# The loads of a fused attention and GELU kernel as steps of their own, and a new order for every block

## The chip, the cores and the metric

The kernel runs on one NeuronCore of a Trainium2 chip. A core has five engines, each with an instruction queue of its own that runs in order: TensorE (PE in the profile; its weight loads are a row of their own, PEld), VectorE (DVE), ScalarE (ACT), GpSimd (POOL) and SyncE (SP). [...]Transfers between HBM and the on-chip memory SBUF run on 16 DMA engines. SP, ACT and POOL issue them: here SP the stores and the transposing loads, POOL the loads that change the type from float32 to bfloat16. The metric is the device time of one execution in microseconds (us), lower is better.

## The reference

Cross-covariance attention over channels, followed by a feed-forward layer with a tanh GELU. There are 4 batches of 6080 tokens with 256 channels; the hidden width is 2048.

```python
qn = q / (np.linalg.norm(q, axis=1, keepdims=True) + 1e-06)      # per channel, over all tokens
kn = k / (np.linalg.norm(k, axis=1, keepdims=True) + 1e-06)
s = kn.transpose(0, 2, 1) @ qn / tau                              # 256 x 256 for each batch
a = softmax(s)                                                    # over the last axis
x = (v @ a).reshape(B * S, D)
h = x @ w_in
g = 0.5 * h * (1.0 + np.tanh(c * (h + 0.044715 * h * h * h)))
out = g @ w_out
```

All the tokens of a batch must have passed through q and k before the first output of that batch can be made.

## The kernel before

The 256 x 256 matrix a is first multiplied into w_in, so each batch has one 256 x 2048 weight AW = a @ w_in (`aw_part`, lines 428 to 436, and `aw_copy`, 438 to 447; steps `aw0` to `aw7` and `ac0` to `ac7`). Then every batch has 12 blocks of 512 tokens (the last has 448), 48 blocks in all. A block n does this:

- v reaches the core in two transfers: `cast_v` (line 133) has POOL copy the float32 rows to a bfloat16 scratch tile `vb` in HBM, and `load_vt` (143) has SP load that transposed into `vT`, one of three buffers.
- h = AW.T @ vT, in pairs of 128-channel slices. Two to eight of the eight pairs are made directly (`mm1`, 484, step `g0` to `g7`: four matmuls of 512 columns into a pair of PSUM banks) and turned into GELU values by ACT (`gelu`, 502, `G0` to `G7`). The other pairs are made two at a time in sets `w0`, `w1`, `w2` by seven half-size products in place of eight (a Strassen scheme; `small`, 542, `w0m1` to `w0m7`), with sums of v made by DVE (`sums_v`, 526, `vs`) and sums of AW (`sums_w`, 513, `SW0` to `SW2`), and copies and additions around them (`set_step`, 580). Blocks 0 and 1 use no set, block 2 one, blocks 3 to 35 two, blocks 36 to 47 three.
- out = g @ w_out, by the same scheme: seven products, each in two halves (`product`, 682, `M1A` to `M7B`), sums of the GELU values by DVE (`sums_1`, 658, `T1a`; `sums_2`, 664, `T2a` to `T4b`), sums of w_out made once at the start (`prep_wout`, 630, `pA11` to `pNA`), additions (`cq`, `y5`, `ap`, `ax`, `c11a`), four turns from columns to rows (`c11`, `c12`, `c21`, `c22`, 719). With the fourth turn of a block SP is given its store, four transfers (782). The last block is stored in halves, `sA` and `sB` (771), from SP and ACT.

While batch b runs its blocks, q and k of batch b + 1 are brought in and reduced, in 8 chunks: `load_one` (95) loads one chunk of q or of k by POOL into one of five buffers; `qsq` and `ksq` (`square`, 167) square it on ACT; `f1` (`fold`, 198) halves the squares on DVE, and `fd` (`fold_dma`, 206) has POOL add them into an accumulator by DMA; `row0` to `row5` (`gram_row`, 217) are the matmuls of k against q. Late in the batch the norms, the softmax and the new AW follow as steps (`fl1`, `gc`, `ss`, `sv`, `pow`, `kf`, `kr`, `krp`, `S0`, `th0`, `dn`, `rc0`, `eT`, `rsum`, `rs`). The first batch's q and k are worked through ahead of the blocks, in the order of lines 794 to 854.

Nothing is scheduled by the framework. Lines 929 to 932 walk through `ORDER[WINDOW[n]]` for each block n, and issue each step as it stands in the text; `-1` and `+1` behind a step name the neighbouring block that it belongs to. This text fixes the order in every engine's queue. `WINDOW` has 48 entries and `ORDER` 31 texts: blocks 8 to 19 and 20 to 33 share texts, as do four blocks near the end.

The transfers hang on three markers in each text, `e0`, `e2` and `e5`, which call `loads` (911): `e0` issues the transpose of block n + 2 and the cast of block n + 3, `e2` the chunk of q with the block's own number in the batch, `e5` the same chunk of k. A gate (`GATE`, 500; `after`, 89) makes each of POOL's loads wait for the last `mm1` or `small` matmul issued ahead of it. Chunk c is so loaded in block c of a batch, and its first `row` or square stands in the next block, for a few chunks in the one after.

Of the kernel before, what the change touches and what calls it, by code (L numbers as in the profile page):

```python
# [18 lines left out]
def kernel(  # L19
# [26 lines left out]
    PE_BLOCKS = 2  # L46
# [611 lines left out]
    def sums_1(n):  # L658
        hc = cols_of(n) // 2
        t1 = t1p.tile([128, 8, BLK // 2], BF16, tag="t1", name=f"t1_{n}")  # L660
        nc.vector.tensor_sub(t1[:, :, :hc], quarter(n, 0, 1), quarter(n, 0, 0))
        TS[n] = {1: t1}

    def sums_2(n, i, half):
        hc = cols_of(n) // 2
        ts = TS[n]
# [127 lines left out]
    with tc.manual_schedule():  # L794
# [78 lines left out]
        def step(what, n):  # L873
# [30 lines left out]
            elif what[0] == "p":  # L904
                prep_wout(what)
            elif what[0] == "e":
                loads(n, int(what[1]))
            else:
                mm2_step(n, what)

        def loads(n, p):
            b, blk = divmod(n, NB)
            gate = GATE[0]
            if p == 0 and PE_BLOCKS <= n + 2 < NN:
                load_vt(n + 2)
            if p == 0 and n + 3 < NN:
                cast_v(n + 3, gate)
            if p in (2, 5) and b + 1 < B and blk < len(chunks_of(b + 1)):
                load_one(b + 1, blk, p // 5, gate)
# [16 lines left out]
    0, 1, 2, 3, 4, 5, 6, 7, 8, 9, 10, 11, 12, 13, 14, 15, 16, 17, 18, 19, 8, 9, 10, 11,  # L936
    12, 13, 14, 15, 16, 17, 18, 19, 8, 9, 20, 21, 22, 23, 24, 25, 26, 27, 27, 27, 27, 28,
    29, 30,
]
ORDER = [  # L940
    """aw4 aw5 aw3 g1 ac3 ac5 aw2 G1 g0 ac2 e0 aw7 G0 g3 ac7 ac4 g2 G3 SW0 e2 aw6 G2 g5 ac6 g4
    T1a G5 vtp G4 g7 vtc1 vtc0 e5 w0m1+2 pA11 G7 g6 pF0 M1A G6 M1B pS1 g1+1 pA12 pF1""",
    """g0 G1 e0 M5B-1 T2a-1 G0 M5A-1 T2b-1 g3 e2 pS2-1 cq-1 g2 T4b-1 G3 T3a-1 M6B-1 G2 M6A-1
    pS3-1 g5 e5 y5-1 ap-1 g4 G5 T3b-1 M7A-1 G4 vs+1 row4 g7 pS4-1 g6 G7 T4a-1 M7B-1 G6 M3A-1
    T1a w0m5+1 row0 w0cq+1 M3B-1""",
    """g0 w0y5 c12-2 ax-2 pNA-2 e0 w0m6 row5-1 w0ap row2-1 M2A-2 qsq M2B-2 w0m2 e2 c11a-2 w0m7
    w0m3 T2b-1 M4B-2 w0Gq M4A-2 w0ax M5A-1 T3a-1 G0 row3-1 M5B-1 T4b-1 w0m4 w0Gx g4 c21-2 w0Gr
    SW1-2 e5 g3 G4 T2a-1 w0m1+1 M1A-1 c22-2 G3 T3b-1 M1B-1 g6 cq-1 y5-1 ksq-1 M6A-1 M6B-1 g5
    ap-1 G6 T1a M3A-1 M7B-1 G5 T4a-1 M7A-1 M3B-1 ksq row1-1 c12-1 g7 ax-1 vs+1 M2A-1 G7 M2B-1
    c11-2 w0m5+1 T2a row2 w0cq+1 M4A-1 T3a M4B-1 w0y5+1 c11a-1 w0m6+1 qsq-1""",  # L950
    """g0 w0ap e0 c21-2 row1-1 w0m7 G0 w0m3 w0ax M1B-1 M1A-1 T2b-1 w0Gx e2 w0m4 row0-1 w0Gr g3
    T4b-1 cq-1 c22-2 w0m2 f1-2 G3 M5A-1 M6A-1 c11-2 M5B-1 fd-2 w0Gq vs+1 w1m1 w1m5 e5 M6B-1
    y5-1 w1cq g4 ap-1 w1y5 T3b-1 w1m6 G4 M3B-1 w1ap M7B-1 row5-1 ksq w1m7 g7 w1ax T1a w1m2 G7
    M3A-1 row4-1 w1m4 w1m3 c12-1 w1Gr M7A-1 w0m5+1 w1Gq ax-1 M2B-1 f1-1 row3-1 w0m1+1 w1Gx
    M2A-1 T4a-1 w0cq+1""",
    """g0 fd-2 T2b-1 w0y5 e0 w0m6 G0 M4A-2 w0ap M4B-2 row3 qsq-1 c21-2 w0m7 g3 e2 w0ax T2a-1 w0m3
    G3 M1B-1 c11a-2 row5 w0m2 T4a-1 row0-1 qsq row4-1 w0m4 T3b-1 M1A-1 vs+1 M5B-1 w0Gr row4 e5
    w1m5 T4b-1 w0Gq row0 row2-1 w1m1 M5A-1 cq-1 row5-1 w1cq g4 w1y5 w1m6 w0Gx M6A-1 w1ap G4
    M6B-1 c22-2 row3-1 w1m7 T3a-1 w1m2 y5-1 w1m3 g7 ap-1 w1Gq w1ax M7A-1 T1a G7 M3B-1 w1m4
    row1-1 w1Gx M7B-1 w1Gr M3A-1 w0m5+1 ksq c12-1""",  # L960
    """g0 T2a-1 e0 w0m1 ax-2 row4 w0cq M2B-2 f1-2 M2A-2 w0y5 row2-1 c11-3 fd-2 G0 w0m6 e2 row2
# [168 lines left out]
```

## Time and profile before

| | |
|---|---|
| median of 13 runs | 716.08 us (710.86 to 721.09) |
| the profiled execution | 721.09 us, the slowest of the 13 |
| its span, first to last instruction | 719.3 us |
| mean granted TensorE clock | 0.989 |
| TensorE busy | 94% of the span |
| ACT, DVE busy | 86%, 85% |
| POOL busy | 13% |
| DMA engines, mean rate | 137 GB/s |

The page of a profile lists the busy time of each engine, the costliest groups of instructions (line, engine, operation, output tile <- input tiles, shape, count, busy time and mean duration in ns), the idle time ahead of a group and what ended it, and the chain of work that ended last, followed back from the last instruction. A timeline gives the instructions of one engine in order: start, length, instruction, and in brackets the idle time before it with its releaser. A matmul on two tiles reads `out<-moving,weights`. `G`, `r`, `p`, `h`, `rb`, `qp` are PSUM tiles: `G` the matrix of k against q, `h` a direct pair, `rb` and `qp` the products of a set, `r` and `p` those of the second layer. `t` is a chunk of q or k, `acc` the accumulator of squares, `ot` a block's output.

The 40 slices of the span show where TensorE is not full:

```profile
PE   3868989998999999999999999999999999999995
DVE  4574867986999878888999878897899999999996
ACT  5356979997888999999888999999888999999993
PEclk9998999999999999999999999999999999999999
DMA  9995697998647899999627797999734736463414
```

Each digit stands for some 18 us, in tenths. The orders begin in the third slice, at about 39 us; the first two are the first batch's q and k. The blocks of batches 0 to 2, up to about 515 us, carry the loads of the next batch in their first eight blocks, and there DMA is high.

### The profile page before, as it was taken

What the parts mean: (1) busy time and instruction counts of PE and PEld (TensorE: products, weight loads), DVE (VectorE), ACT (ScalarE), POOL (GpSimd) and SP (SyncE); (2) the same over time, 40 slices, a digit from 0 to 9 for tenths busy, and PEclk for the clock granted to TensorE, in tenths of its full rate; (3) what the DMA queues carried; (4) which work ended last, traced back from release to release, by engine and by line L of the source; (5) the groups of instructions that cost most, each with busy time, mean ns of one, the idle gap of its engine ahead of it and who ended that gap; (6) DMA issues with size and microseconds to landing.
All of it is one profiled execution on the core that took longest, in us unless ns stands there. A gap on an engine that the chain in (4) does not pass through costs nothing.

```text
span 719.3 us, 14365 instructions
## 1 busy us (share of the span) xinstructions
PE 679.5 (94%) x5479; PEld 531.5 (74%) x5479; DVE 609.0 (85%) x1180; ACT 619.0 (86%) x894; POOL 92.0 (13%) x155
## 2 busy tenths in 40 slices
PE   3868989998999999999999999999999999999995
PEld 2635757785777877777777778777777888888884
DVE  4574867986999878888999878897899999999996
ACT  5356979997888999999888999999888999999993
POOL 4310111121100111121100011112010000000000
PEclk9998999999999999999999999999999999999999
DMA  9995697998647899999627797999734736463414
GB/s 242 208 241 84 99 178 153 204 174 169 116 69 107 148 176 162 223 176 200 124 50 109 136 201 142 188 201 194 150 60 67 109 58 97 80 117 59 73 31 86
DMA packets 165734, 98.21 MB, mean 137 GB/s; under 512 B 150848, under 2 KB 153664, under 8 KB 164672
## 3 DMA queue, kind: packets, MB, share of 16 engines
q0 software_dynamic: 16896, 58.34, 43.2%
q1 hardware_dynamic: 147664, 37.67, 31.3%
q10 hardware_dynamic: 1104, 1.28, 0.5%
q8 instruction: 43, 0.70, 0.4%
q14 instruction: 27, 0.22, 0.1%
HBM read 78.91 MB, written 36.83 MB: 161 GB/s over the span
## 4 chain that ended last, share of the span: by engine, by line
PE 81%; DMA 9%; issue 7%; POOL 1%; DVE 1%; ACT 0%; POOLq 0%; DVEq 0%
PE r L700 21%; PE h L494 17%; PE p L700 16%; PE rb L570 12%; PE qp L570 9%; DMA t<-in_k_dram 7%; PE G L225 4%; PE awp L434 1%; DMA t<-in_q_dram 1%; POOL t L99 1%; POOL vb L138 0%; PE ss L257 0%; POOL wst L622 0%; PE rk L379 0%; DVE a L191 0%
## 5 line engine op out<-in xcount | busy, mean ns | idle before, releaser
L700 PEld LDWEIGHTS <-wcomb 128*128 128x128 bf16 x2688 | 263.3, 98 | 44.8 <-issue 1.7
L504 ACT ACTIVATE g<-h 128x1024 bf16<-128x1024 f32 (+1 forms) x178 | 179.3, 1014 | 34.6 <-PE h L494 32.3
L494 PE MATMUL h<-vT,aw 128*128 128x512 bf16 (+1 forms) x648 | 165.0, 378 | 0.0
L700 PE MATMUL r<-t,wcomb 128*128 128x256 bf16 (+1 forms) x1152 | 164.7, 271 | 0.3 <-DVE c L716 0.2
L596 ACT ACTIVATE g<-qp 128x1024 bf16<-128x1024 f32 (+1 forms) x103 | 104.5, 1016 | 6.1 <-PE qp L570 4.7
L494 PEld LDWEIGHTS <-aw 128*128 128x128 bf16 x712 | 70.2, 99 | 50.3 <-issue 1.9
L700 PE MATMUL p<-g,wcomb 128*128 128x256 bf16 (+1 forms) x760 | 104.6, 272 | 0.0
L570 PEld LDWEIGHTS <-sw 128*128 128x128 bf16 x824 | 80.7, 98 | 21.2 <-issue 0.6
L178 ACT ACTIVATE sq<-t 128x1536 bf16<-128x1536 bf16 (+4 forms) x60 | 80.8, 1358 | 13.0 <-DMA t<-in_q_dram 9.8
L591 DVE TENSOR_TENSOR qp<-rb,yw 128x512 f32<-128x512 f32 (+1 forms) x103 | 71.1, 690 | 20.8 <-PE rb L570 10.4
L594 DVE TENSOR_TENSOR xw<-rb,yw 128x512 f32<-128x512 f32 (+1 forms) x103 | 69.7, 677 | 20.5 <-PE rb L570 18.6
L570 PE MATMUL rb<-tv,sw 128*128 128x256 bf16 (+1 forms) x412 | 78.5, 273 | 0.0
L570 PEld LDWEIGHTS <-aw 128*128 128x128 bf16 x618 | 60.1, 98 | 23.2 <-issue 8.5
L225 PE MATMUL G<-t 128*128 128x256 bf16 (+1 forms) x368 | 62.2, 276 | 10.5 <-DMA t<-in_k_dram 10.5
L673 DVE TENSOR_TENSOR t<-g,t 128x1024 bf16<-128x1024 bf16 (+1 forms) x96 | 63.5, 672 | 7.6 <-ACT g L504 6.4
L586 ACT ACTIVATE qp<-rb 128x512 f32<-128x512 f32 (+1 forms) x103 | 60.3, 585 | 10.5 <-PE rb L570 5.3
L138 POOL DMA_DIRECT2D vb<-in_v_dram x46 | 25.0, 544 | 330.4 <-PE h L494 280.4
L589 ACT ACTIVATE yw<-qp 128x512 f32<-128x512 f32 (+1 forms) x103 | 61.1, 593 | 4.6 <-PE qp L570 2.1
L675 DVE TENSOR_TENSOR t<-g 128x1024 bf16<-128x1024 bf16 (+1 forms) x96 | 64.2, 671 | 0.2
L677 DVE TENSOR_TENSOR t<-t,g 128x1024 bf16<-128x1024 bf16 (+1 forms) x96 | 64.0, 670 | 0.0
L604 ACT ACTIVATE g<-xw 128x512 bf16<-128x512 f32 (+1 forms) x103 | 63.1, 624 | 0.2 <-DVE xw L594 0.2
L601 ACT ACTIVATE g<-rb 128x512 bf16<-128x512 f32 (+1 forms) x103 | 61.3, 596 | 1.8 <-PE rb L570 0.9
(122 smaller groups left out, 901.5 us busy)
## 6 DMA issues: line engine op xcount, KB each, us to landing
out_dram<-ot SPq DMA_DIRECT2D x176, 128.0 KB, 3.1
acc<-a POOLq DMA_DIRECT2D x24, 768.0 KB, 7.0
vb<-in_v_dram POOLq DMA_DIRECT2D x42, 256.0 KB, 4.7
t<-in_q_dram POOLq DMA_DIRECT2D x22, 384.0 KB, 6.5
t<-in_k_dram POOLq DMA_DIRECT2D x22, 384.0 KB, 6.5
wst<-in_moe_w_out_dram POOLq DMA_DIRECT2D x2, 1024.0 KB, 11.4
t<-in_q_dram POOLq DMA_DIRECT2D x3, 512.0 KB, 15.1
t<-in_k_dram POOLq DMA_DIRECT2D x3, 512.0 KB, 17.0
```

The source lines that it names most:

```text
L178: nc.scalar.activation(o, t[:np_, r, :], AF.Square)
L225: nc.tensor.matmul(G[b][:, jc, :], lhsT=qt[:np_, r, jc * 128 : jc * 128 + 128], rhs=kt[:np_, r, :], start=first and jc == 0, stop=jc == 1, ...
L494: mm = nc.tensor.matmul(hp[:, u, :cols], lhsT=AW[b][:, cc, fc * 128 : fc * 128 + 128], rhs=vt_tiles[n][:, cc, :cols], start=cc == 0, stop= ...
L504: nc.scalar.activation(gs(n)[:, 2 * p : 2 * p + 2, :cols], HP.pop((n, p))[:, :, :cols], AF.Gelu_apprx_tanh)
L570: GATE[0] = nc.tensor.matmul(acc[:, u * hc : u * hc + hc], lhsT=lhs[:, u * 128 : u * 128 + 128], rhs=rhs, start=m in (1, 5) and u == 0, st ...
L591: nc.vector.tensor_add(qp(n, i)[:, 1, :c], RB[n, i][:, :c], YW[n, i][:, :c])
L594: nc.vector.tensor_add(XW[n, i][:, :c], RB[n, i][:, :c], YW.pop((n, i))[:, :c])
L596: nc.scalar.activation(gs(n)[:, 2 * pa : 2 * pa + 2, :c].rearrange("p u (t x) -> p t u x", t=2), QP.pop((n, i))[:, :, :c].rearrange("p t ( ...
L673: nc.vector.tensor_sub(o, quarter(n, 1, 1, f0, f1), ts[1][:, f0:f1, :hc])
L675: nc.vector.tensor_sub(o, quarter(n, 1, 1, f0, f1), quarter(n, 0, 1, f0, f1))
L677: nc.vector.tensor_sub(o, ts[2][:, f0:f1, :hc], quarter(n, 1, 0, f0, f1))
L700: nc.tensor.matmul(ACCS[n, acc][:, :hc], lhsT=wcomb[:, w, fc, :], rhs=x, start=first and k == 0, stop=k == 3, skip_group_check=True)
```

## The change

The markers and `loads` go. In their place are four steps with a block number like any other: `lt` (transpose of v), `lv` (cast of v), `lq` and `lk` (a chunk of q, of k). With a block number m of the batch, `lq` and `lk` load chunk m - 1 of the next batch; `lq+2` in block n is so chunk n + 1, where before it was chunk n. Batch 1's chunks 0 to 3 are loaded in the same blocks as before (written `+1`), the `lq` of chunk 4 follows in block 3, its `lk` and chunk 5 in block 4, chunk 6 in block 5, chunk 7 in block 6. For batches 2 and 3, chunk 0 is loaded in the block ahead of the ones that carried the loads before (blocks 11 and 23), chunk 7 in blocks 18 and 30. `lq` stands about a third, `lk` about two thirds into a block; `lt+2` and `lv+3` stay near its start. The gates stay.

All other steps are the same, one by one, but every block has a text of its own now, and so another order. Block 0 begins with `aw2 aw3 g0` in place of `aw4 aw5 aw3 g1` and no longer reads block 2's `vT`; the sums of w_out begin at its end. The end of block 47 is another. Two lines allow `T3a` ahead of `T1a` of its block.

```diff
     def sums_1(n):
...
-        TS[n] = {1: t1}
+        TS.setdefault(n, {})[1] = t1
     def sums_2(n, i, half):
...
-        ts = TS[n]
+        ts = TS.setdefault(n, {})
...
-            elif what[0] == "e":
-                loads(n, int(what[1]))
+            elif what == "lt":
+                load_vt(n)
+            elif what == "lv":
+                cast_v(n, GATE[0])
+            elif what in ("lq", "lk"):
+                load_one(b, c, "qk".index(what[1]), GATE[0])
...
-        def loads(n, p):
-            b, blk = divmod(n, NB)
-            gate = GATE[0]
-            if p == 0 and PE_BLOCKS <= n + 2 < NN:
-                load_vt(n + 2)
-            if p == 0 and n + 3 < NN:
-                cast_v(n + 3, gate)
-            if p in (2, 5) and b + 1 < B and blk < len(chunks_of(b + 1)):
-                load_one(b + 1, blk, p // 5, gate)
...
 WINDOW = [
-    0, 1, 2, 3, 4, 5, 6, 7, 8, 9, 10, 11, 12, 13, 14, 15, 16, 17, 18, 19, 8, 9, 10, 11,
-    12, 13, 14, 15, 16, 17, 18, 19, 8, 9, 20, 21, 22, 23, 24, 25, 26, 27, 27, 27, 27, 28,
-    29, 30,
+    0, 1, 2, 3, 4, 5, 6, 7, 8, 9, 10, 11, 12, 13, 14, 15, 16, 17, 18, 19, 20, 21, 22, 23,
+    24, 25, 26, 27, 28, 29, 30, 31, 32, 33, 34, 35, 36, 37, 38, 39, 40, 41, 42, 43, 44,
+    45, 46, 47,
 ]
 ORDER = [
-    """aw4 aw5 aw3 g1 ac3 ac5 aw2 G1 g0 ac2 e0 aw7 G0 g3 ac7 ac4 g2 G3 SW0 e2 aw6 G2 g5 ac6 g4
-    T1a G5 vtp G4 g7 vtc1 vtc0 e5 w0m1+2 pA11 G7 g6 pF0 M1A G6 M1B pS1 g1+1 pA12 pF1""",
-    """g0 G1 e0 M5B-1 T2a-1 G0 M5A-1 T2b-1 g3 e2 pS2-1 cq-1 g2 T4b-1 G3 T3a-1 M6B-1 G2 M6A-1
-    pS3-1 g5 e5 y5-1 ap-1 g4 G5 T3b-1 M7A-1 G4 vs+1 row4 g7 pS4-1 g6 G7 T4a-1 M7B-1 G6 M3A-1
-    T1a w0m5+1 row0 w0cq+1 M3B-1""",
...
-    M5B T2a w2Gr M1B w1Gr T3a M1A M5A cq T2b y5 M6A T3b M6B c22-1 M2A y6 c11-1 T4b M7A M7B T4a
-    M2B ax c11a M4B c11 M4A c22 M3B c21 M3A sB a12 c12 sA""",
+    """aw2 aw3 g0 ac3 lt+2 lv+3 g1 ac2 G0 SW0 aw5 G1 aw4 ac5 g2 lq+1 ac4 g3 G2 aw6 G3 aw7 ac6 g4
+    ac7 g5 T1a G4 lk+1 vtp G5 g6 vtc0 pA11 g7 G6 vtc1 T2a M1B G7""",
+    """g0 pF0-1 lt+2 lv+3 M1A-1 G0 pS1-1 g1 pF1-1 cq-1 M5B-1 G1 g2 T2b-1 M5A-1 G2 pS2-1 g3 lq+1
+    pS4-1 y5-1 M6B-1 G3 g4 T3a-1 T4b-1 M6A-1 G4 g5 ap-1 pS3-1 pA12-1 M3B-1 M3A-1 G5 T4a-1 g6
+    c12-1 lk+1 pNA-1 M7A-1 T3b-1 g7 vs+1 G6 M7B-1 w0m1+1 G7 ax-1 row2 M2B-1 T1a M4B-1 ksq
+    M2A-1 M4A-1 c11a-1 w0m5+1 c21-1""",
...
+    """g0 w2Gr-1 c22-2 M4B-2 c11a-2 G0 w0m5 T2a-1 w0m1 M4A-2 w0cq M5B-1 c21-2 w0y5 w0m6 c11-2
...
+    w2m6 M7A-1 w0Gx w2ap M3A-1 g3 c12-1 ax-1 w2m7 w2m2 G3
+    c22-1 w2m3 M2A-1 w2ax M4B-1 w1Gx T1a M4A-1 w2Gq M2B-1 c21-1 w2m4 w2Gx w1m4 c11a-1 M1A w2Gr
+    c11-1 M1B w1Gr T2a M5B cq M2A T2b M6A T3a M6B T3b M5A y6 M2B T4b y5 M7B T4a M7A M3B ax M3A
+    c11a M4A c11 M4B c22 c21 a12 sB c12 sA""",
 ]
```

## The prediction

> **What bounds the kernel now.** I read the page first, then TensorE's timeline for every idle stretch over a quarter of a microsecond, then the windows around these with the granted clock, then the chain of waits and SP's queue at the end. The page's first part says which engine sets the time:
>
> ```profile
> PE 679.5 (94%) x5479; PEld 531.5 (74%) x5479; DVE 609.0 (85%) x1180; ACT 619.0 (86%) x894; POOL 92.0 (13%) x155
> ```
>
> TensorE is busy for 679.5 of 719.3 us, but busy is not yet full speed. The windows (columns: stretch, its length, busy us of PE, PEld, DVE, ACT and POOL, granted clock, DMA share, GB/s) separate the two:
>
> ```profile
> 54.28:61.10 6.82, 5.11 (x18) 2.60 (x19) 1.72 (x3) 1.97 (x2) 0.00 (x0) 0.50 0.31 57
> 105.48:108.90 3.42, 3.33 (x12) 1.76 (x12) 2.28 (x5) 0.57 (x1) 0.33 (x2) 0.50 1.08 265
> 166.92:170.33 3.41, 2.94 (x15) 2.08 (x14) 0.18 (x1) 1.58 (x2) 0.00 (x0) 0.50 1.16 279
> 180.00:490.00 310.00, 309.91 (x2484) 241.96 (x2483) 275.73 (x540) 287.12 (x411) 42.63 (x70) 1.00 0.82 149
> ```
>
> Between 180 and 490 us TensorE loses 0.09 us: there the order leaves nothing but the matmuls. ACT (287.1 of 310) and DVE (275.7) keep up with 7% and 11% to spare. In the three short stretches it runs at half clock. Each follows one of the idle stretches in TensorE's timeline (start, length, instruction, in brackets the idle time before it and what ended it):
>
> ```profile
> 39.62 1.46 PE L434 MATMUL awp<-win_bf,eT 128*128 128x512 bf16 x6 [1.32 <-DMA win_bf<-in_moe_w_in_dram]
> 55.99 0.59 PE L570 MATMUL rb<-vT,aw 128*128 128x256 bf16 x2 [7.11 <-DMA vT<-vb]
> 105.57 0.59 PE L225 MATMUL G<-t 128*128 128x256 bf16 x2 [3.46 <-DMA t<-in_k_dram]
> 167.39 1.44 PE L225 MATMUL G<-t 128*128 128x256 bf16 x6 [3.56 <-DMA t<-in_k_dram]
> 502.02 0.82 PE L225 MATMUL G<-t 128*128 128x256 bf16 x6 [1.74 <-DMA t<-in_k_dram]
> ```
>
> So the recoverable time is a few waits for transfers, not work. The chain of waits gives the transfers' own times, to be held against the usual landing time in the list of DMA issues (6.5 us):
>
> ```profile
> 93.49 12.04 DMA t<-in_k_dram
> ...
> 154.46 12.89 DMA t<-in_k_dram
> ...
> 491.89 10.09 DMA t<-in_k_dram
> ```
> ```profile
> t<-in_k_dram POOLq DMA_DIRECT2D x22, 384.0 KB, 6.5
> ```
>
> A load of k that has 9 us before its first matmul is hidden when it takes 6.5 us and shows when it takes 12. The end is not TensorE's: its last matmul ends at 711.9, and SP's queue is still issuing:
>
> ```profile
> 701.08 13.11 SPq L789 DMA_DIRECT2D out_dram<-ot  x8
> 714.32 2.09 SPq L778 DMA_DIRECT2D out_dram<-ot  x4
> ```
>
> The last block's results are turned by 712.85, but SP works through the store of the block before it until 714.19, and only then issues the last four pieces, which land by 718.15.
>
> **What the Trainium skill says.** "TensorE: Matmul & The Clock Gate", Part 1 (the clock gate): after about one idle window of 3.4 us the clock goes to half, in free-running windows of 3413 ns. The trace agrees: the waits of 7.11, 3.46 and 3.56 us are followed by 6.82, 3.42 and 3.41 us at 0.50, and the one of 1.74 us by none. The same page (architectural detail) calls ACT and DVE strict FIFO and lets PE pull only weight loads ahead; so a matmul placed ahead of its data holds everything behind it, as the 7.11 us shows. "DMA: Bandwidth & Descriptors", Rules for kernel authors: issue a DMA early and wait late; and, under "Issuing engines are not separate DMA queues", all queues share the same 16 engines, which is why a load takes 12 us beside stores and accumulations here.
>
> **The change part by part.** All steps of before are in after, each once, for the same blocks, apart from the load markers; so TensorE's work is equal. I count places in the order in TensorE time: four 512-column matmuls take 0.86 us and four of 256 columns 0.44 us less rounding (0.108 each), as the chain shows, and the steps between two places are added up. The orders hold 641.6 us of such work.
>
> *Block 0 and 1, vT of block 2.* Before, the first matmul on it (w0m1+2) stands in block 0, 5.7 us after the place of its transpose; it landed at 55.86. After, no step reads it until vs+1 in block 1, 19.1 us after that place. TensorE enters the orders at about 38.4 (below), the transpose's place is 2 us later, so vs is due at 59.5 and the vT is 3.6 us early. Gained: 7.11, and of the 5.11 us of work done at half clock one half, 2.56. Sum 9.7.
>
> *First steps.* aw4 waited for the third piece of w_in (1.32 us, landed 39.48). After, aw2 and aw3 come first and read the second piece, landed 38.22. TensorE starts near 38.4 in place of 39.62: 1.2.
>
> *Loads of q and k.* Before, k's lead (place of load to first reader) is 8.6 to 17.9 us, and 8.8, 9.1 and 9.1 for the three that showed. After it is 17.3, 23.3 and 21.8 for these, and 17 or more for all but the first three chunks of batch 1 (13.7, 10.1, 14.9; k of the first two landed within 6.6 us of issue, and 10.1 is the weak one). The longest landing of these three was 12.9. All three waits go: 3.46 plus half of 3.33; 3.56 plus half of 2.94; 1.74. Sum 5.1 + 5.0 + 1.7 = 11.9. POOL issues the same 60 loads at about 0.55 us; at 13% busy that is free. The five buffers of q and k hold: the slot is last read 17 us or more before a load wants it. No gate is new: each load still waits for the last matmul ahead of it, and behind it on POOL stand a cast of v (9.6 us or more ahead of its transpose) and a fold.
>
> *The end.* The store of block 46 gets its fourth turned piece 2.2 us earlier in the order (2.7 us before the last matmul's place before, 4.9 after). SP is then free when the last halves come. After TensorE's last matmul come c21, a12 and c12 (0.4 us each, 1.2) and the four pieces with about 3 us to landing and issue: 4.2, where before 711.9 to 718.15 is 6.3. Gained 2.0; bounds 0 (SP still late) and 2.6.
>
> *New steady orders.* Blocks 8 to 19 and the last batch's had shared orders; after, each has its own. What they could lose is not shown by before. I counted, for every matmul on a sum of DVE and every reuse of a PSUM pair, the lead behind its producer: medians of before and after differ little (T2a to its first product 4.1 and 3.9 us, T3b 3.45 and 3.45, pair 1 1.29 and 1.51), and the smallest are of one size. So I take nothing there; bounds 0 and, at 0.1 us a block, 4.
>
> *A residue.* Blocks 0 to 2 lose the pause in which DVE and ACT caught up. Before, at 49 to 56 us DVE made four weight sums of w_out while TensorE stood:
>
> ```profile
> 49.33 1.22 DVE L635 TENSOR_TENSOR wf<-wst,wst 128x1024 f32<-128x1024 f32 x1
> 50.58 0.69 DVE L637 CAST wcomb<-wf 128x1024 bf16<-128x1024 f32 x1
> ```
>
> w_out's second half landed at 48.73. After, the product that needs that cast (M5B) is due at 38.4 + 10.4 + 2.2 = 51.0, and the cast can be done at 50.65: 0.35 us to spare. Block 1 gives DVE 14.3 us of instructions by their means, 12.9 when I shorten them by the tenth by which DVE's back-to-back means overlap; begun at 48.7, done at 61.6, where TensorE wants to leave the block at 62.0. This fits, with no slack. I book 3 us for it and for late landings elsewhere, from 0 to 10.
>
> **Sum.** 9.7 + 1.2 + 11.9 + 2.0 = 24.8; less the residue 3 is 21.8. The profiled execution took 721.09 us, so after is 699.3: I say 699. The 13 runs have a median of 716.08; the profiled one is their slowest. I read the 5 us between them as longer waits in that execution, which the change would remove too, so I do not subtract again: against the median the gain is 17, or 2.4%.
>
> **The rivals.**
> *The first blocks turn into a wait of DVE.* For it: the 0.35 us above, and DVE's full block 1. Against: by the count above each product still has its data just before its place. If w_out lands 3 us later or DVE needs a tenth more, TensorE waits about 5 us more and loses 1.7 to the half clock: 699 + 6.7 = 706.
> *The loads are no earlier on the chip.* For it: POOL's queue is in order, and at 491.89 the k load came behind a fold (accumulation) which had kept POOL 9.9 us for DVE. If folds hold POOL before each load, the leads shrink and the 11.9 stay: 711. Against: a fold stands just behind its DVE sum in both orders, and a lead of 20 us outlasts 9.9 plus 6.5.
> *Slower: the DMA engines run full.* In 240 to 300 us they are busy for 0.92 of the time. After, batch 1's chunks 3 to 7 are loaded within blocks 3 to 6, ten loads in place of eight, and every load block issues two pairs' worth of reads ahead of need. If transposes of v then take over 15 us (their longest before; leads after are 13.2 us and up), the matmuls on vT wait in each of 24 load blocks. At 0.86 us a block this costs 20.7 us, the point from which the kernel is slower by 0.5% (719.7). Against: in batches 2 and 3 no byte is added or crowded, and before had no wait for vT after block 2.
>
> **How the numbers follow.** 0.5% (3.6 us) is about what a measurement of this kernel tells from no change. Forecast 0.64, at 694 to 702; DVE in the first blocks 0.19, 702 to 709; loads no earlier 0.10, 709 to 714, of which half lies over 712.5; slower 0.07, of which 0.01 ends within 0.5%. So faster 0.88, same 0.06, slower 0.06. The range is 693 to 710, from all gains and no residue (696.3) less some scatter, up to the end of the second case.
>
> **What would show it.** Right: no idle over 2 us in TensorE's timeline after 40 us; no stretch at half clock before the end; the L225 group without a DMA releaser; SP's last issue within 3 us of the last matmul. DVE's rival: an idle stretch at 50 to 62 us ended by DVE. Loads no earlier: L225 still ended by in_k_dram. Slower: L570 or L532 ended by DMA vT, block after block. Wrong altogether: many idle stretches of ACT or DVE origin between 180 and 490 us.

## The result, and the profile after

The changed kernel took 711.72 us in the median of 11 runs (703.51 to 726.25), beside 716.19 for the kernel before on the same chip; the ratio is 0.9895, 95% interval 0.9863 to 0.9927. So it is faster by 1.0% (by 0.6% in the medians), where 2.4% was forecast. Here and below, medians and ranges are over all runs, while a ratio leaves out runs over 1.5% above the fastest of their kernel, and so flatters a kernel that stalls in some of its runs. The profiled execution took 711.72 us itself; its span is 709.7 us, against 719.3 before.

First the page of the profile after: busy time of the engines, the chain of waits by engine and by line, and two groups of instructions.

```profile
PE 680.6 (96%) x5479; PEld 533.2 (75%) x5479; DVE 609.7 (86%) x1180; ACT 618.5 (87%) x894; POOL 90.9 (13%) x155
...
PE 88%; DMA 9%; DVE 2%; issue 0%; ACT 0%; POOL 0%; DVEq 0%; POOLq 0%
PE r L700 22%; PE h L494 20%; PE p L700 17%; PE rb L570 12%; PE qp L570 9%; PE G L225 4%; DMA vT<-vb 4%; DMA t<-in_k_dram 2%; PE awp L434 2%; DMA acc<-a 1%; DMA t<-in_q_dram 1%; PE ss L257 0%; DVE ot L725 0%; PE ss L250 0%; DVE t L675 0%
...
L700 PE MATMUL r<-t,wcomb 128*128 128x256 bf16 (+1 forms) x1152 | 163.7, 273 | 6.6 <-DVE t L675 6.6
...
L225 PE MATMUL G<-t 128*128 128x256 bf16 (+1 forms) x368 | 61.1, 278 | 0.7 <-DMA t<-in_k_dram 0.7
```

The waits on k (L225) are down from 10.5 us to 0.7. In their place `vT<-vb`, the transpose of v, holds 4% of the chain, and the products `r` show an idle time ended by DVE. TensorE's timeline between 100 and 190 us has just two idle stretches over a microsecond:

```profile
133.41 1.87 PE L700 MATMUL r<-t,wcomb 128*128 128x256 bf16 x8 [6.56 <-DVE t L675]
179.17 1.87 PE L257 MATMUL ss<-ones_f,acc 128*128 128x1 f32 x8 [2.56 <-DVE acc L215]
```

The windows (columns as before: length, busy us of PE, PEld, DVE, ACT, POOL, granted clock, DMA share, GB/s) show what follows each, and that the long middle is as full as before:

```profile
131.30:138.10 6.80, 4.69 (x19) 2.64 (x19) 5.17 (x12) 1.02 (x1) 0.00 (x0) 0.50 1.17 227
179.10:185.90 6.80, 6.73 (x28) 4.69 (x29) 4.99 (x13) 1.60 (x3) 1.05 (x1) 0.50 0.46 80
190.00:490.00 300.00, 299.99 (x2404) 233.95 (x2402) 265.63 (x517) 279.95 (x398) 43.65 (x73) 1.00 0.84 151
```

DVE is only the last link. Its own timeline at the two places shows what it waited for:

```profile
131.68 0.42 DVE L532 TENSOR_TENSOR tv<-vT 128x512 bf16<-128x512 bf16 x1 [7.26 <-DMA vT<-vb]
...
177.50 0.69 DVE L215 TENSOR_TENSOR acc<-acc 128x512 f32<-128x512 f32 x1 [3.67 <-DMA acc<-a]
```

and the chain of waits names the transfers with their durations:

```profile
104.45 27.21 DMA vT<-vb
131.65 0.02 issue
131.68 0.44 DVE tv L532
...
132.71 0.66 DVE t L675
...
133.41 1.87 PE r L700 x8
...
167.31 10.16 DMA acc<-a
177.47 0.02 issue
177.50 0.69 DVE acc L215
```

The sum of v (`vs`, L532) for block 7 stands in DVE's queue ahead of a sum of GELU values (L675), and that one is what TensorE's product needs: DVE's order passes the wait on. The transpose took 27.2 us; the longest of before was 15.0. What was in flight beside it is in the view of the DMA engines between 100 and 132 us (40 slices of 0.8 us; each digit is the busy share in tenths):

```profile
DMA  9999999999919900000064197968999999999999
GB/s 127 142 254 284 276 253 247 207 210 249 486 25 260 65 16 16 16 12 13 16 28 20 12 52 56 87 82 146 204 236 224 190 146 190 203 192 199 211 227 273
...
acc<-a POOLq DMA_DIRECT2D x2, 768.0 KB, 14.9
...
vT<-vb SPq DMA_TRANSPOSE x1, 27.2
```

For seven microseconds the packets that began amount to 12 to 28 GB/s in place of some 200. The view counts a packet in the slice in which it began, so the digits read 0 though the engines were not idle: in the trace, twelve packets of 6144 bytes that began between 110.0 and 110.9 us were under way until 118 to 121, up to 10.6 us each. Packets of this size are those of the folds (`acc<-a`, the DMA that adds squares into the accumulator): 3072 of them for 24 folds, 384 in a kernel with three. This fold was issued at 106.40, two microseconds behind the transpose. It took 20.1 us itself.

At the end, SP's queue:

```profile
689.92 15.11 SPq L789 DMA_DIRECT2D out_dram<-ot  x5
705.13 2.03 SPq L778 DMA_DIRECT2D out_dram<-ot  x4
```

The last matmul ends at 702.5, SP has the store of block 46 in hand until 705.0, and the last pieces land at 708.5: 6.0 us behind the matmul, where before it was 6.2. The 15.1 us of the first line are mostly waiting: it joins the last piece of block 45, at 689.92, to the four of block 46. Of these SP issued three from 697.72 to 699.13 and the fourth only at 704.71. In the trace the fourth waits for a semaphore (a counter on which instructions wait) that ACT's first piece of block 47 also counts up; that piece was issued at 702.99 and landed at 704.70. Before, the same pair stands at 713.86 (landing) and 713.88 (issue).

### The profile page after: what moved, and what is told of

Its sections match the earlier page's. It is cut to its first block, busy times and chain, and to the rows that moved or that the text cites. A ratio compares the mean times of both kernels' runs of the same rounds, so it can differ in the third digit from the quotient of the medians.

```text
span 709.7 us, 14328 instructions
## 1 busy us (share of the span) xinstructions
PE 680.6 (96%) x5479; PEld 533.2 (75%) x5479; DVE 609.7 (86%) x1180; ACT 618.5 (87%) x894; POOL 90.9 (13%) x155
## 4 chain that ended last, share of the span: by engine, by line
PE 88%; DMA 9%; DVE 2%; issue 0%; ACT 0%; POOL 0%; DVEq 0%; POOLq 0%
PE r L700 22%; PE h L494 20%; PE p L700 17%; PE rb L570 12%; PE qp L570 9%; PE G L225 4%; DMA vT<-vb 4%; DMA t<-in_k_dram 2%; PE awp L434 2%; DMA acc<-a 1%; DMA t<-in_q_dram 1%; PE ss L257 0%; DVE ot L725 0%; PE ss L250 0%; DVE t L675 0%
## 5 line engine op out<-in xcount | busy, mean ns | idle before, releaser
L700 PE MATMUL p<-g,wcomb 128*128 128x256 bf16 (+1 forms) x760 | 108.7, 273 | 0.1
L591 DVE TENSOR_TENSOR qp<-rb,yw 128x512 f32<-128x512 f32 (+1 forms) x103 | 71.0, 689 | 17.5 <-PE rb L570 12.6
L594 DVE TENSOR_TENSOR xw<-rb,yw 128x512 f32<-128x512 f32 (+1 forms) x103 | 69.7, 677 | 10.6 <-PE rb L570 9.8
L570 PEld LDWEIGHTS <-aw 128*128 128x128 bf16 x618 | 60.4, 98 | 12.5 <-issue 0.2
L586 ACT ACTIVATE qp<-rb 128x512 f32<-128x512 f32 (+1 forms) x103 | 59.9, 582 | 10.6 <-PE rb L570 6.2
L675 DVE TENSOR_TENSOR t<-g 128x1024 bf16<-128x1024 bf16 (+1 forms) x96 | 64.0, 671 | 0.0
L225 PE MATMUL G<-t 128*128 128x256 bf16 (+1 forms) x368 | 61.1, 278 | 0.7 <-DMA t<-in_k_dram 0.7
```

The source lines that it names most:

```text
L225: nc.tensor.matmul(G[b][:, jc, :], lhsT=qt[:np_, r, jc * 128 : jc * 128 + 128], rhs=kt[:np_, r, :], start=first and jc == 0, stop=jc == 1, ...
L570: GATE[0] = nc.tensor.matmul(acc[:, u * hc : u * hc + hc], lhsT=lhs[:, u * 128 : u * 128 + 128], rhs=rhs, start=m in (1, 5) and u == 0, st ...
L591: nc.vector.tensor_add(qp(n, i)[:, 1, :c], RB[n, i][:, :c], YW[n, i][:, :c])
L594: nc.vector.tensor_add(XW[n, i][:, :c], RB[n, i][:, :c], YW.pop((n, i))[:, :c])
L675: nc.vector.tensor_sub(o, quarter(n, 1, 1, f0, f1), quarter(n, 0, 1, f0, f1))
L700: nc.tensor.matmul(ACCS[n, acc][:, :hc], lhsT=wcomb[:, w, fc, :], rhs=x, start=first and k == 0, stop=k == 3, skip_group_check=True)
```

## The experiments

In the short diffs a line is a block, the step, and the step that it stands ahead of. Ratios are to the kernel before on the same chip.

**Which crowd: loads or folds.** Four kernels from the changed one: batch 1's loads spread, its folds moved away from the transposes, both, and its folds left out.

```diff
 k1_spread
-3: lq+2  w1m7
+4: lq+1  M5A-1
-5: lk+2  w1m1
+6: lk+1  g3
...
 k2_folds
-3: fd-1  cq-1
+3: fd-1  row4-1
-5: fd-1  w0m1
+5: fd-1  w1cq
-6: fd-1  w0m6
+6: fd-1  g4
-7: fd-1  M1B-1
+7: fd-1  g4
-9: lt+2  w1Gx-1
+9: lt+2  vs+1
```

> The changed kernel with batch 1's chunks 4 to 7 of q and k spread: one load per about 6.2 us of TensorE work in place of one per 4.9, nothing else moved. Theory crowding (the ten loads packed into blocks 3 to 6 fill the DMA engines, so the transpose of v issued at 104 us took 27 us): that transpose lands in under 12 us, the 6.6 us wait of TensorE at 133 us and its 6.8 us at half clock go, the time falls by some 10 us to about 702. Theory fold beside transpose (an accumulating DMA issued 1 to 2 us behind a transpose of v holds both): the transpose of block 5 still takes over 15 us and the time stays within 3 us of 711.7. Theory chance: a freeze of this size comes at another place or not at all, whatever is moved; medians stay near 711.

> The changed kernel with batch 1's folds of blocks 3, 5, 6 and 7 moved from 1 to 4 us behind the transpose of v to the middle of the block, and block 11's transpose moved 6 us later so that it doesn't start with the last fold; loads as in the changed kernel. Theory fold beside transpose: no transpose of v takes over 12 us in blocks 3 to 10, both waits (6.6 us at 133, 2.6 us at 179 us) and their half-clock stretches go, the time falls by about 15 us to some 697. Theory crowding: the transpose issued in block 5 still takes 20 us or more and DVE still waits for it; only the wait at 179 us may go, about 6 us, giving 706. Theory chance: near 711.

> Both edits together, the loads spread and the folds and block 11's transpose moved. Either theory: no long transposes and no wait over 2 us on TensorE after 40 us, 696 to 700. If the gain is that of one of the two edits alone, that one carries the cause; if each gives half, both do. Theory chance: near 711 still.

> The changed kernel without six of batch 1's eight folds (the accumulating DMAs of chunks 1 to 6 are left out, so that batch's norms are not those of the reference); loads and transposes where they were. Theory fold beside transpose: transposes of blocks 3 to 8 take 6 to 8 us, no wait at 133 us, about 702 (the one at 179 us may stay). Theory crowding by loads alone: the block 5 transpose still takes over 12 us, though less than 27, since a fold's bytes are missing too; DVE waits 2 us or more for it. Theory chance: near 711.

| | median us | runs, lowest to highest | ratio, 95% |
|---|---|---|---|
| k1_spread | 705.45 | 4, 698.21 to 709.13 | 0.9829 (0.9753 to 0.9904) |
| k2_folds | 697.76 | 4, 696.36 to 701.05 | 0.9758 (0.9696 to 0.9820) |
| k3_both | 700.59 | 4, 697.17 to 703.67 | 0.9793 (0.9738 to 0.9849) |
| k4_nofold | 700.12 | 4, 696.73 to 702.98 | 0.9786 (0.9729 to 0.9843) |

k1_spread still has both waits, smaller, in TensorE's timeline, and its transposes issued from 90 to 124 us still took 13.9 to 16.0 us:

```profile
126.13 0.59 PE L225 MATMUL G<-t 128*128 128x256 bf16 x2 [4.61 <-DMA t<-in_k_dram]
...
176.06 1.05 PE L257 MATMUL ss<-ones_f,acc 128*128 128x1 f32 x8 [1.85 <-DVE acc L215]
```

k2_folds has none over 0.4 us there (one of 1.67 us comes later, at 443.52), and its window is full:

```profile
100.00:190.00 90.00, 89.89 (x717) 69.51 (x715) 79.95 (x155) 83.93 (x121) 12.87 (x20) 1.00 0.83 151
```

Two of its transposes there took 13.0 and 14.2 us, over the 12 that were expected, the second with a fold 0.2 us behind it: the order had put the two apart, the queues brought them together. Both fitted into their leads. k4_nofold tells loads from folds best: all loads of the changed kernel are in place, and with the six folds gone its transposes from 91 to 159 us took 3.9 to 8.4 us. Its one wait over 0.5 us after 40 us, of 2.31 us at 444.83, lies in batch 3, whose folds it keeps.

So the order of four folds and one transpose is worth what the forecast missed. The medians do not rank k2, k3 and k4 (their intervals overlap): what is left differs from run to run. Nor is the gain of k1_spread over the changed kernel clear, since its runs lie within 698 to 709 us and those of the changed kernel begin at 703.51.

**Only the two places where it showed.** m4_two keeps the edits of k2_folds in blocks 5 and 9 alone.

> The changed kernel with two edits of k2_folds alone: the fold of block 5 goes from 0.6 us behind that block's transpose of v to the middle of the block, and block 9's transpose goes some 6 us later, away from block 8's last fold. The folds of blocks 3, 6 and 7 stay 1 to 4 us behind their transposes. Theory (these two collisions made the two waits of 6.6 and 2.6 us with their half-clock windows): 697 to 702 us, no wait over 1 us between 100 and 185 us. Rival (the folds of blocks 3, 6 and 7 keep the DMA engines back too and another transpose comes late in their place): a wait of 2 us or more on vT or on a load between 100 and 185 us, 704 to 710 us.

704.14 us (697.24 to 706.73), ratio 0.9828 (0.9767 to 0.9889). The half on the places holds: no wait between 100 and 185 us. The time does not, since in the profiled run another transpose, of batch 3, took 24.8 us. The line of TensorE's timeline, then that of the chain:

```profile
447.66 0.58 PE L570 MATMUL rb<-tv,aw 128*128 128x256 bf16 x2 [5.84 <-DVE xw L594]
```
```profile
421.12 24.79 DMA vT<-vb
```

That transpose has a fold at 424.4 beside it and loads on both sides. It is the place that cost k2_folds 1.67 us. The changed kernel has the collision in more than one place, and which of them stalls is not the same in each run; what the folds of blocks 3, 6 and 7 are worth this run does not tell.

**Making the collision where there was none.**

```diff
-14: fd-1  ap-1
+15: fd-2  T3a-1
-15: lq+2  T3b-1
+15: lq+2  lv+3
-15: fd-1  w1y5
+16: fd-2  lv+3
...
```

> k2_folds with the collision made anew in batch 2, where it had none: in four blocks (15 to 18) the fold's accumulating DMA is issued just behind the transpose of v, and the load of q just behind the fold, as in block 5 of the changed kernel. Leads of the transposes there are 18 to 26 us. Theory (fold and load behind a transpose hold all three back): in these four blocks the transposes of v, near 198, 212, 226 and 240 us, take 15 us or more against 6 to 9 in k2_folds, and the folds 13 or more; where one takes longer than its lead, DVE's sum of v waits and TensorE with it; 700 to 706 us if one or two show. Rival (the crowd of batch 1's ten loads in four blocks is what it needs, or it was chance): transposes stay below 12 us, no wait, 697 to 700 us.

703.24 us in the median of 20 runs, from 696.33 to 719.05. (The places in the expectation are in the order's TensorE time; in the trace they lie some 40 us later.) The first three transposes took 13.5, 12.6 and 26.3 us (at 241.5, 256.7 and 270.2), where those of k2_folds took 7.2, 5.8 and 9.5. In the trace the fold stands ahead of each, not behind, by 2.2, 3.7 and 2.2 us, since SP came to its transpose later than POOL to the fold; these folds took 8.6, 10.1 and 12.5 us. In k2_folds they already stood 7.2, 4.9 and 2.2 us ahead. What came nearer in all three is the load of q, from 4.6 to 6.2 us behind the transpose to 1.4 to 2.6. So this run shows what a load does beside a fold and a transpose, and does not tell what the fold adds.

The fourth was pushed to 298.7 by SP's queue, 17 us behind its fold, and took 5.4. The 26.3 us fitted into its lead, but a wait came later. TensorE's timeline, then DVE's:

```profile
324.49 1.01 PE L700 MATMUL r<-t,wcomb 128*128 128x256 bf16 x4 [3.48 <-DVE p L750]
```
```profile
322.42 0.43 DVE L532 TENSOR_TENSOR tv<-vT 128x512 bf16<-128x512 bf16 x1 [4.00 <-DMA vT<-vb]
```

This transpose took only 8.2 us, but was issued as late as 314.15, when its cast of v had landed (314.10). POOL had issued no transfer from 282.4 to 302.0: the next in its queue was a fold, which waited for the one of 281.48 to land, 20.0 us after its issue; the cast stood behind it. A held fold delays the loads and casts behind it on POOL as well.

Of the four transposes one took over 15 us and three 12.6 or more: the crowd makes a stall likely, not certain. 14 of these 20 runs took over 700 us, and 2 of 10 of k2_folds (on two other chips).

**Moving the rest apart.** n1_best issues eight more transposes 2 to 6 us later and moves one more fold.

> k2_folds with the remaining collisions taken apart as well: the transposes of v of blocks 3, 17, 18, 20, 21, 27, 32 and 33 are issued 2 to 6 us later in their block, and the fold of block 28 moves to the middle of it, so that by the order no fold stands within 3.7 us of a transpose of v (k2_folds: nine stand within 3.3 us). Theory (a fold, two loads and a transpose of v in flight together is what holds transposes for 15 us and more): no transpose over 13 us after 60 us, no idle stretch of TensorE over 1 us between 40 and 690 us, every run between 695 and 700 us, median 697. Rival (such stalls come by chance wherever the DMA engines are full): one transpose or more over 15 us again and runs spread from 696 to 706 us, median 699 to 702.

701.91 us, six runs from 697.13 to 717.12: the rival's median, and a wider spread than it said. SP's queue and TensorE's timeline tell why:

```profile
100.12 11.01 SPq L789 DMA_DIRECT2D out_dram<-ot  x4
111.23 6.12 SPq L148 DMA_TRANSPOSE vT<-vb  x1
```
```profile
134.42 1.86 PE L700 MATMUL r<-t,wcomb 128*128 128x256 bf16 x8 [7.20 <-DVE t L675]
```

The issues of the four stores ahead of the transpose kept SP for 11 us, so it began at 111.23, 0.07 us ahead of a fold (111.30), and took 21.4 us. The DMA engines were full in that stretch (share 1.07); that this is what held the stores is likely, and not shown. The order fixes who stands behind whom in one queue, but not when SP's queue meets POOL's.

**What of the fold it is.** Two kernels from the changed one. n2_nofolds keeps only the first, plain fold of each batch; n3_plain keeps all of them, without the addition.

```diff
-        nc.gpsimd.dma_start(out=ACC[b], in_=FOLD.pop((b, c)),
-                            **({} if first else {"accum_op": ALU.add}))
+        nc.gpsimd.dma_start(out=ACC[b], in_=FOLD.pop((b, c)))
```

> The changed kernel with all accumulating folds left out, in every batch: only the first of each batch, a plain copy, is issued, so the sums of squares for q and k of batches 1 to 3 lack seven of eight chunks; DVE's sums, all loads, casts and transposes stay where the changed kernel has them. Theory: no transpose over 11 us after 60 us, no wait over 1 us, 695 to 699 us, all runs within 3 us. Rival (loads, casts, stores and transposes crowd each other without folds): a transpose over 15 us near 104 or 421 us, and 702 us or more.

> The changed kernel with the folds' DMAs as plain writes: same tiles, bytes, places and waits, but each overwrites the accumulator and adds nothing, so the sums of squares of batches 1 to 3 are those of one chunk. Theory (it is the accumulation, which holds an engine for up to 10 us a packet, that stalls the transpose): folds land in 3 to 6 us, no transpose over 12 us, 696 to 702 us. Rival (their traffic alone, whatever they do with it): a transpose of 15 us or more beside a fold, a wait on vT or acc, 706 to 714 us as in the changed kernel.

n2_nofolds: 697.14 us, 696.96 to 697.94, ratio 0.9719 (0.9664 to 0.9773). n3_plain: 696.83 us, 696.58 to 698.08, ratio 0.9718 (0.9654 to 0.9782). With every other transfer of the changed kernel in place, the time is that of k2_folds' better runs and the spread is 1 to 1.5 us. The longest transpose without folds took 10.9 us. With plain folds one took 18.5, beside two folds and three loads at 103 us, and fitted into its lead; so plain writes can slow it too. The DMA view of n3_plain, 100 to 132 us:

```profile
GB/s 146 161 323 434 310 319 220 195 228 435 90 131 22 23 24 28 27 28 88 41 70 202 364 363 237 186 207 220 238 214 210 359 64 331 356 351 175 204 240 262
...
acc<-a POOLq DMA_DIRECT2D x2, 768.0 KB, 11.3
```

The trough is there, 5 us long in place of 7. Between 60 and 500 us the 6144-byte packets of the folds took 268 ns in the mean and 1.9 us at most as plain writes, and 445 ns and 10.6 us with the addition. The mean is 267 and 268 ns in the two traces with plain folds, and 377 to 445 ns in the fourteen with adding ones. The Trainium skill ("DMA: Bandwidth & Descriptors", Rules for kernel authors) says that an accumulating DMA reads its destination and writes it later. That fits a longer packet; that it is the reason for the stall no run here shows.

All traces together, transposes issued after 60 us; a fold or load is counted as near when it is in flight at the transpose's issue, or is issued within 8 us after it:

```
14 traces with adding folds:    no fold, fewer than two loads   251 transposes, longest  9.0 us,  0 over 12
                                no fold, two or more loads       92 transposes, longest 12.1 us,  2 over 12
                                a fold, fewer than two loads     61 transposes, longest 12.8 us,  5 over 12
                                a fold and two or more loads    199 transposes, longest 27.2 us, 39 over 12
2 traces with plain folds:      a fold and two or more loads     26 transposes, longest 18.5 us,  2 over 12
4 traces, folds left out or added by an engine:                 172 transposes, longest 11.7 us,  0 over 12
```

Folds alone and loads alone seldom do it; both together do, in one transpose of five. Whether plain folds do it less often the 26 cannot tell; the run times can: the four of n3_plain lie within 1.5 us.

**Are the leads of the loads worth anything by themselves?** m2_oldloads and n4_best_oldloads put the loads back to one chunk a block with leads of 7 to 18 us; o2_before_plain takes the addition out of the kernel before.

> k2_folds (697.8 us when it ran) with the loads of q and k put back to about where before had them: of the same block's chunk, one chunk of q and k a block, q some 3 us and k some 6 us into the block, leads of 7 to 18 us to the first reader in place of 17 to 24. Folds stay where k2_folds has them. Theory A (the lead of the loads is worth its 11.9 us by itself): two to four waits of 2 to 4 us on L225 ended by the load of in_k_dram, each with a half-clock window behind it, 705 to 711 us. Theory B (the loads of before landed late because folds and transposes of v ran together; with the folds moved away a load lands in 6 to 9 us and the short lead is enough): no wait over 1 us, 697 to 701 us.

> n1_best with the loads of q and k back where the kernel before has them by time within the block (one chunk a block, leads to the first reader of 7 to 18 us in place of 17 to 24). Theory A (the leads are worth their 11.9 us by themselves): waits of 2 us and more on L225 ended by the load of in_k_dram, 702 to 709 us. Theory B (loads land late only where a fold and a transpose hold the DMA engines; with these apart a short lead is enough): a median within 2 us of n1_best's, and no wait on L225 over 1 us.

> The kernel before with the folds' DMAs as plain writes that overwrite the accumulator (sums of squares of batches 1 to 3 are those of one chunk); its loads, orders and the wait in block 0 stay. Theory B (before's three waits on k's loads come from the adding DMAs too): these three waits are gone or under 1 us, the wait of 7 us in block 0 stays, 704 to 707 us against some 716. Theory A (they come from the short leads alone): waits of 2 us and more on L225 near 105 and 167 us stay, 712 to 717 us.

n4_best_oldloads: 698.64 us (697.23 to 703.48), no wait over 1 us in its profile from 40 us on, a median under n1_best's by 3.3. m2_oldloads: 701.22 us (696.88 to 707.92); its profile has one wait on a load. TensorE's timeline and the chain:

```profile
434.62 0.58 PE L225 MATMUL G<-t 128*128 128x256 bf16 x2 [8.25 <-DMA t<-in_k_dram]
```
```profile
413.62 20.95 DMA t<-in_k_dram
```

That load lay beside a fold (410.0, 8.7 us) and a transpose (410.2) that took 22.6. o2_before_plain: 713.41 us (710.31 to 717.16), ratio 0.9964 (0.9942 to 0.9986). Of the three waits on k two shrink to 0.58 and 0.52 us, and one stays; the time is the one that theory A gave. Timeline and chain (L224 is the L225 of the others, one line up):

```profile
101.76 0.59 PE L224 MATMUL G<-t 128*128 128x256 bf16 x2 [2.98 <-DMA t<-in_k_dram]
```
```profile
90.15 11.56 DMA t<-in_k_dram
```

So both theories hold a part. In the orders of k2_folds and n1_best short leads are mostly enough. In those of before, two of the three waits go with the adding folds; the first, on a load with 8.8 us to its reader, stays beside a plain fold as well (11.56 us). In the kernel before, too, the fold beside that load is the batch's first, which adds nothing. Leads of 17 us and more are an insurance that pays only when something stalls.

**The wait in block 0 alone.** The kernel before with one step moved.

```diff
-0: w0m1+2  pA11
+1: w0m1+1  w0m5+1
```

> The kernel before with one step moved: the first matmul on vT of block 2 (w0m1+2, last third of block 0) goes to the end of block 1, just ahead of its sister w0m5. Nothing else changes. Theory (the prediction's term for block 0: 7.11 us of waiting and half of 5.11 us of work at half clock): some 9.7 us less than before, 705 to 707 us; no idle stretch over 1 us in TensorE's timeline between 50 and 65 us, no stretch at half clock there; the two waits on k's loads near 105 and 167 us stay. Rival (DVE used that pause to catch up on the sums of w_out, the prediction's own worry): a wait ended by DVE takes its place between 50 and 62 us and half or less is gained, 710 to 713 us.

706.86 us in the median of 17 runs against 716.67: 9.8 us, ratio 0.9850 (0.9824 to 0.9877). Nothing is idle over 0.5 us between 44 and 64 us, so no wait for DVE took its place. The waits on k stay, all three: 3.31 us at 95, 2.81 at 156 and 1.74 at 491.

**Adding without a DMA.** The folds added by GpSimd in SBUF, in the changed kernel and in m1_block0, and by DVE.

```diff
-        nc.gpsimd.dma_start(out=ACC[b], in_=FOLD.pop((b, c)),
-                            **({} if first else {"accum_op": ALU.add}))
+        t = FOLD.pop((b, c))
+        if first:
+            nc.gpsimd.dma_start(out=ACC[b], in_=t)
+        else:
+            nc.gpsimd.tensor_add(ACC[b], ACC[b], t)
```

> The changed kernel with the folds (but the first of each batch, a plain copy) added by a GpSimd instruction in SBUF, acc = acc + a1 over 128x1536, in the place of the DMA that adds. Theory (only the adding DMA stalls the transposes): as without folds, 696 to 698.5 us, every run within 3 us, no transpose over 12 us. GpSimd is 13% busy; the add's price is not in a trace so far: DVE's smaller sum of this tile takes 0.94 us, so 1 us below and, if GpSimd is six times slower, 6 us above, 21 adds, 21 to 126 us of a queue that has some 600 us free. Rival (the adds hold GpSimd's queue before loads and casts, or slow DVE beside them): waits on L225 or waits ended by DVE return, 700 to 708 us.

> The kernel before with two edits only: the step w0m1+2 from block 0 to block 1 (as in m1_block0) and the folds added by GpSimd (as in o1_pool). Loads of q and k, steady orders and the end stay as before has them. Theory B: both large terms come without the change's loads, 697 to 701 us, no wait over 1 us between 50 and 690 us. Theory A: the waits on k's loads stay, 705 to 708 us as m1_block0.

> The changed kernel with the folds (but the first of each batch, a plain copy) added by DVE, acc = acc + a1 over 128x1536 in f32. DVE's 128x512 sum in f32 takes 0.69 us, so some 2 us each, 21 of them, 43 us more on an engine that is busy 610 of 710. Theory (no adding DMA, no stalls, but DVE's queue is held 2 us at a time, where its leads before TensorE are 1.3 to 4 us): no transpose over 12 us, small waits ended by DVE in the blocks that fold, 698 to 706 us. Rival (DVE has too little to spare in these blocks): waits of over 1 us in most of them, 707 to 720 us.

All three are slower than before, and than both theories had it: 727.71 us (ratio 1.0173, 1.0141 to 1.0204), 737.63 (1.0331, 1.0282 to 1.0380) and 723.73 (1.0108, 1.0084 to 1.0131). The transposes are short (longest 11.7 us), yet DVE pays. GpSimd's timeline in o1_pool, then DVE's:

```profile
99.35 3.11 POOL L215 TENSOR_TENSOR acc<-acc,a 128x1536 f32<-128x1536 f32 x1
```
```profile
99.56 4.00 DVE L664 TENSOR_TENSOR t<-g 128x2048 bf16<-128x2048 bf16 x1
```

The subtraction takes 1.21 us in the mean of the changed kernel and 4.00 here. It ends 1.1 us behind GpSimd's addition, as if it had got on only after that. The Trainium skill ("GPSIMD Engine Reference", 1. Specifications) has GpSimd's SBUF interface shared with VectorE, with contention for instructions with two SBUF inputs; this is such a one. On DVE the add takes 1.75 us in the mean in place of my 2, but it stands ahead of sums that TensorE waits for:

```profile
81.94 0.38 PE L573 MATMUL rb<-tv,aw 128*128 128x256 bf16 x2 [1.86 <-DVE xw L597]
```

o4_b0_pool, which has the loads of before, tells something of the loads too. Two of the three waits on k are gone from it, and the first is there, with no adding DMA in the kernel:

```profile
95.15 0.38 PE L228 MATMUL G<-t 128*128 128x256 bf16 x2 [3.25 <-DMA t<-in_k_dram]
```

An addition by DMA costs the engines no more than its issue on GpSimd, 0.9 us, and that is still the cheapest of the three ways in this kernel.

**The two orders once more, on one chip.**

> k2_folds once more, unchanged. Theory (moving four folds and one transpose takes the usual stalls away, and leaves those of batch 3 to chance): median 697 to 701 us, lowest near 696.4, one run in four over 702, some 12 us under the changed kernel on the same chip. Rival (its first four runs were lucky, the stalls move elsewhere as in n1_best): median over 703.

> The changed kernel once more, unchanged. Theory (its stall in block 5 is near certain): no run under 703, median 709 to 713 us, highest over 718. Rival (the stall comes by chance in it too): at least one run in five at 696 to 700.

k2_folds: 697.16 us, ratio 0.9714 (0.9668 to 0.9760), five of six runs between 696.65 and 697.52, one at 709.21. The changed kernel: 707.62 us, ratio 0.9812 (0.9744 to 0.9880), six runs from 698.75 to 712.14. It was said that no run would be under 703; two were, one of them under 700. Here the median lies within the range of the prediction; that is the luck of which runs stalled, not the forecast's merit. The profiled one, of 698.75 us, has the same pair in block 5 (transpose at 106.0, fold 1.1 us later), taking 16.5 and 15.4 us, which its lead of some 20 us covers. So k2_folds beats both kernels by some 10 and 19 us in the median.

## Why the prediction was wrong

| term of the sum | forecast, us | shown, us |
|---|---|---|
| block 0, vT of block 2 | 9.7 | 9.8 in m1_block0; no such wait in the profile after |
| first steps | 1.2 | 1.9: first `awp` at 37.77 in place of 39.62, of which 0.4 is an earlier start of the steps ahead |
| waits on k's loads | 11.9 | 11.9 in the two profiles: 0.7 left on L225, none over 0.4 |
| the end | 2.0 | 0.2: last landing 6.0 us behind the last matmul, before 6.2 |
| residue | -3 | -14.8 |

The residue is 6.56 us idle and half of 4.69 at half clock (2.35), and 2.56 idle and half of 6.73 (3.37). The sum is 9.0; the two spans differ by 9.6, so 0.6 are not placed. The prediction's condition for half clock, one idle window of 3.4 us, is too strict for these runs: the 2.56 us were followed by 6.8 us of it, and the 1.85 us of k1_spread by 3.4, while 2.21 us in o1_pool (at 115.88) were followed by none.

**The term that failed** is "A residue. ... I book 3 us for it and for late landings elsewhere": mis-sized by a factor of five, and looked for in the wrong place. The prediction put it with DVE in the first blocks, where nothing came: after 40 us the first idle stretch over 1 us is at 127. It came from late landings, the transpose of block 5 and the last fold of the batch.

**The mechanism was in the text, under the slower rival** ("the DMA engines run full", "if transposes of v then take over 15 us"), at 7%, priced as a stall in each of 24 blocks. It came in one or two places of a profile, where it came at all. Its "Against" looked at bytes per batch, and batch 1's loads, which it did name, are only part: k1_spread took their crowding away and left transposes of 14 to 16 us. What the prediction did not price is the fold. It wrote that "a fold stands just behind its DVE sum in both orders", which is so; but the new texts of blocks 3, 5, 6 and 7 put it 1 to 4 us behind the transpose, and the profile of before already hinted at what that does: its transposes of 12.1, 13.6 and 15.0 us all had a fold within 6 us. The leads of 13.2 us and up were counted against a longest of 15, as if that were a property of transposes and not of what lay beside them.

**The loads' term was right in size for the profiled run and half right in cause.** For two of the three waits longer leads were one cure of two, since they go as well when the folds do not add by DMA; the first stays in the order of before without any adding DMA, and there only the lead or another order is a cure. That the 5 us between the profiled execution and the median of before were longer waits fits this and is not shown, since before has one profile. The floor that the sum gave, 696.3 us, is near what the kernels without stalls reach (medians of 697.14 and 696.83 in n2_nofolds and n3_plain), so not subtracting those 5 us again was right; that it fits to a microsecond is in part luck, since the end gave 1.8 us less than booked and the first steps 0.7 more.

**The end.** The store of block 46 does come earlier: its first piece goes out 4.8 us ahead of the last matmul's end, before 3.1. But its fourth waits, as before, for the landing of a piece that ACT stores after the last matmul. So SP is late all the same: the bound of 0 that the prediction named, by a wait that it had not seen.

**The other rivals.** DVE in the first blocks: no. Loads no earlier: no, L225 lost its waits. New steady orders at 0: 190 to 490 us lose 0.01 us, so yes.

## What to carry to other kernels

When a transfer is late, list what is in flight beside it before giving it more lead: here 39 of the 46 transposes over 12 us had a fold and two or more loads near them, and moving four folds and one transpose took away most of what was left to gain. Price the waits of a slack order by the longest landing under the new neighbours, not by the longest in the old profile, and keep in mind that two queues in order do not keep their distance in time once one of them is held up. Where single runs of a kernel spread by 10 us or more and the rest agree, look for a stall that comes by chance, and judge by many runs. And read a merged line of a queue as a span, not as work: the 15 us of SP at the end were in the main a wait for results and one for a semaphore shared with another queue.

## What was unexpected of the hardware

- A fold with addition (768 KB, 6.9 us in the median) and a transpose of v issued within 2 us took 20.1 and 27.2 us together, with loads beside them; the packets that began in 7 us of that amount to 12 to 28 GB/s for all 16 engines. Why they stood so long is open.
- The same folds without addition in the same places (n3_plain) left no wait of TensorE over 0.4 us after 40 us in the profile: the median went from 711.7 to 696.8 us, and the spread of the runs from 23 us (11 runs) to 1.5 (4 runs).
- SP can be held by its own issues: in n1_best a transpose of v took it 8.9 us to issue, where 1.5 is usual, and four stores 11.0, so that later transfers start late.
- A GpSimd addition of 3.1 us went with a DVE subtraction beside it of 4.0 us in place of 1.2.
